# Two-stage fused attention and two-layer MLP: the order of all parts written out letter by letter

## Chip, cores and metric

The kernel runs on one core of one Trainium2 chip. The metric is the device time of one execution in microseconds, lower is better. Before the change it is 1310.85 us, the median of 3 runs (1309.78 to 1312.3).

## The reference, cut to what matters

`x` has shape (8, 8, 512, 64) and `state` (8, 8, 32, 64), both float32; the weights are float64 in memory.

```python
scores = scale * x @ state^T;  a = softmax(scores);   xread = a @ state
scores2 = scale * state @ x^T; a2 = softmax(scores2); sread = a2 @ x
t = concat([xread, sread], axis=2) as 4608 tokens of 512
h = (t @ w1) * (t @ w2) @ w3          # (512,1024), (512,1024), (1024,1024)
y = h @ w_out                          # (1024,512)
g = y @ w_in2; g = g - tanh(g)         # (512,2048)
out = g @ w_out2                       # (2048,512)
```

## The kernel before

**Stages.** Eight blocks `b` of 512 tokens hold what x reads, and a ninth (8) of 256 tokens what the state reads. Up to stage 2 there are four kinds of work. *Decoding* turns a float64 weight, read as two 32-bit words, into float32 (`unpack_abs` L343 and mostly `unpack_tail` L346 on ScalarE; `unpack_clamp`, `unpack_shift`, `unpack_end` L362 to L380 on VectorE; some tails on VectorE too). *The w3 products* multiply w3 and w_out: 16 items `t`, each with four turns on TensorE (`w3_turn` L771), a copy on ScalarE (L840), and four products with 512 columns (`w3_mul` L780; the first eight items need item `j` of both weights decoded). *Attention* (`attn_parts` L458): turn x, scores, two softmaxes, `sread`. *Folds* (`fold` L917) multiply the state by w1 and w2; the results go to DRAM (`fold_store` L952) and come back per block and `k` as `m` (`load_m` L1009). *Stage 1* (`stage1` L1036) multiplies `m` by the attention weights, *stage 2* (`stage2` L1069) the result by the w3 products. Stages 3 and 4 (L1295 to L1394) run after that in an order of their own, which the change leaves alone. Every stage matmul is done in three passes on a high and a low half.

**What sets the order.** Nothing is issued at once. Each helper calls `part` (L391), which puts a part on one of 13 streams with its engine (PE, ACT, DVE, SP), its cost in ns, what it needs and makes, and which ring of buffers it takes and gives back. `Plan.run` (L203) then makes eight rounds: `order` (L146) plays the streams by those costs and takes, for the engine that is free first, the part with the earliest due time; `justify` (L172) finds due times backwards. The round with the earliest end of PE is issued, part by part. Each engine executes its own parts strictly in that order, SyncE's DMA issues included, and `Plan.place` also picks the PSUM bank. The costs are `COST`, `WHOLE`, `TURN` (L36 to L42) and, for a change of kind on TensorE (turn, tiled for folds, scores and sread, whole for the rest), `SWITCH` (L45). DMAs are costed by their bytes.

**Around the change.** `units` (L799) says how w3 and w_out items 0 to 7 are decoded: items 0 and 1 one by one, then 2 and 3, 4 and 5, 6 and 7 in pairs. `load_xn` (L449) brings a block of x in four transfers of 256 KB, one for each `c`. The ring `m` has three buffers, `ph` four, `w3t` four; four PSUM banks `acc0` to `acc3` accumulate and four others are shared. The first TensorE instruction of the program is the turn of w3 item 0.

Of the kernel before, what the change touches and what calls it, by code (L numbers as in the profile page):

```python
# [18 lines left out]
P = 128  # L19
# [19 lines left out]
}  # L39
PASS = 226.7  # L40
WHOLE = 867.0
# [4 lines left out]
    ("whole", "tiled"): 91.0, ("turn", "tiled"): 91.0, ("tiled", "turn"): 97.0,  # L46
    ("tiled", "whole"): 230.0, ("turn", "whole"): 52.0, ("whole", "turn"): 10.0,
}


class Plan:
# [60 lines left out]
    def place(self, p, t):  # L112
# [5 lines left out]
        if p["bytes"]:  # L118
            self.moved = max(self.moved, end + 600) + p["bytes"] / 365.0
            end = self.moved + 2500  # L120
# [25 lines left out]
    def order(self):  # L146
        self.clear()
        found, lists = [], [list(s["parts"]) for s in self.streams]
        while any(lists):
            can = []  # L150
            for s, parts in zip(self.streams, lists):
                seen = set()
                for k, p in enumerate(parts[:s["ahead"]]):
                    if p["eng"] not in seen:
                        seen.add(p["eng"])
                        t = self.start(p)
                        if t is not None:
                            can.append((t, p["late"], parts, k, p))
            if not can:
                left = [parts[0] for parts in lists if parts]  # L160
                assert not left, [(p["eng"], p["need"], p["take"]) for p in left]
            t0, _, _, _, p0 = min(can, key=lambda c: c[0])
            t, _, parts, k, p = min(
                (c for c in can if c[4]["eng"] == p0["eng"] and c[0] <= t0 + self.NEAR),
                key=lambda c: (c[1] + self.CHANGE * (c[4]["kind"] not in (None, self.kind)), c[0]),
            )
            del parts[k]
            self.place(p, t)
            found.append(p)
        return found  # L170

    def justify(self, found):  # L172

        end = max(p["span"][1] for p in found)
        gaps = {e: [(0.0, end)] for e in self.REACH}
        bound = {id(p): end for p in found}
        for s in self.streams:
            last = {}
            for p in s["parts"]:
                if p["eng"] in last:  # L180
                    p["after"].append(last[p["eng"]])
                last[p["eng"]] = p
        late = {}
        for p in sorted(found, key=lambda p: -p["span"][1]):
            free = gaps[p["eng"]]
            k = next(
                (
                    k for k in reversed(range(len(free)))
                    if min(free[k][1], bound[id(p)]) - free[k][0] >= p["dur"]
                ),  # L190
                0,
            )
            a, b = free[k]
            t = min(b, bound[id(p)]) - p["dur"]
            free[k:k + 1] = [(a, t), (t + p["dur"], b)]
            late[id(p)] = t
            for q in p["after"]:
                lag = q["lag"] if q["eng"] != p["eng"] or q["bytes"] else 0.0
                bound[id(q)] = min(bound[id(q)], t - lag)
        for p in found:  # L200
            p["late"] = late[id(p)]

    def run(self):  # L203
        for s in self.streams:
            for p in s["parts"]:
                p["late"] = s["rank"].get(p["eng"], 9) if p["rank"] is None else p["rank"]
        best = None
        for _ in range(self.ROUNDS):
            found = self.order()
            end = max(p["span"][1] for p in found if p["eng"] == "PE")  # L210
            if best is None or end < best[0]:
                best = end, [(p, p["banks"]) for p in found]
            self.justify(found)
        for p, banks in best[1]:
            self.picked += banks
            p["fn"]()
# [3 lines left out]
def tile_kernel(  # L220
# [160 lines left out]

    plan = Plan()
# [8 lines left out]
    def part(stream, eng, cost, fn, need=(), make=(), take=(), give=(), size=0, rank=None, kind="whole"):  # L391
        if isinstance(cost, tuple):
# [21 lines left out]

    acc = {}

    def bank(t, name):
        acc[t] = pacc.tile([P, 512], F32, tag=f"acc{t}", name=name)

    with ExitStack() as actx:  # L420
# [28 lines left out]
        def load_xn(b):  # L449
            if b < B:  # L450
                t = pt.tile([P, NC, H, D], F32, tag="xn", name=f"xn{b}", bufs=2)
                xn[b] = t.rearrange("p c h d -> p c (h d)")
                for c in range(NC):
                    nc.sync.dma_start(
                        t[:, c], x[b].rearrange("h (p c) d -> c p h d", c=NC)[c]
                    )

        def attn_parts(b):  # L458
# [146 lines left out]
            def p(eng, cost, f, v=(), need=(), make=(), take=(), give=(), size=0, kind="turn"):  # L605
                part(
                    a_s, eng, cost, later(f, *v), [(b, *n) for n in need], [(b, *n) for n in make],
                    [(t, (b, *k), u) for t, k, u in take], [(b, *g) for g in give], size,
# [9 lines left out]
            if b == 0:  # L618
                p("SP", 3500, load_xn, (0,), (), [("xn",)], [("xn", ("xn",), KT + G)], (), 1 << 20)
# [22 lines left out]
            for j in range(G):  # L642
                p("DVE", full, by_head, (j,), [("sc", j)], [("a", j)], [("xt", ("a", j), 1)])
                p("DVE", 900, max2, (j,), [("sc", j)], [("m2", j)])
                p("ACT", 900, exp2, (j,), [("m2", j), ("a", j)], [("e", j)])
# [11 lines left out]
            for j in range(G):  # L657
                p("DVE", 1100, sum1, (j,), [("ex", j)])
# [8 lines left out]
                p("DVE", 330, whole2, (j,), [("e", j)], [("r2", j)])  # L667
                p("DVE", full, lo, (j,), [("hi", j)], [("at", j)], (), [("at32", j)])
            for j in range(G):
# [5 lines left out]
                    "DVE", 230, srtake, (j,), [("sr", j), ("r2", j)], [("srb", j)],  # L675
                    [("srb", ("srb",), 1)] if j == 0 else (), [("sr_ps", j)],
                )
            if b + 1 < B:
                part(
                    a_s, "SP", 3500, later(load_xn, b + 1), [], [(b + 1, "xn")],  # L680
                    [("xn", (b + 1, "xn"), KT + G)], (), 1 << 20,
# [14 lines left out]
        for b in range(B):  # L696
            if b % 4 == 0:
                r = b // 4
                part(
                    f_s, "SP", 4900, later(load_rows, r), [], [("zst", r)],  # L700
                    [("zst", ("zst", r))], (), 1 << 18,
# [78 lines left out]
        def w3_mul(t):  # L780
            h, j = divmod(t, nj)
            v = w3v[t]
            for a in range(4):
# [15 lines left out]
        units = [(half, (i,)) for i in range(2) for half in range(2)]  # L799
        units += [(half, (i, i + 1)) for i in range(2, nj, 2) for half in range(2)]  # L800
        f32_of = {(half, i): ("f32", half, items) for half, items in units for i in items}
        for u, (half, items) in enumerate(units):
            for i in items:
                part(
                    w_s, "SP", 450, later(fetch, i, half), (), [("raw", i, half)], (), (), 1 << 19
                )
        for t in range(2 * nj):
# [19 lines left out]
            if t in (0, 1, nj, nj + 2):  # L827
                u = nj + (t if t < nj else t // 2 - 2)
                part(
                    w_s, "SP", 450, later(fetch, u, 0), (), [("raw", u, 0)],  # L830
                    [("praw", ("praw", u))], (), 1 << 20,
# [4 lines left out]
                [("w3x", ("w3x", t), 1), ("w3t", ("w3t", t))],  # L836
# [6 lines left out]
            part(  # L843
                x_s, "PE", 4 * WHOLE, later(w3_mul, t),
                [("w3t", t), f32_of[1, j]], [("mul", t)],
                [(f"acc{a}", ("w3o", h, a), 2) for a in range(4)] if j == 0 else (), [("w3t", t)],
            )
            if j == nj - 1:
                for a in range(4):
                    part(  # L850
                        x_s, "ACT", ("scalar", 512), lambda h=h, a=a: copy(*w3_slice(h, a)[1::-1]),
                        [("mul", t)], [("w3oh", h, a)], (), [("w3o", h, a)],
# [15 lines left out]
        part(x_s, "SP", 0, open_pa, [("mul", 2 * nj - 1)], ["pa"])  # L868
# [27 lines left out]
        for k in range(NK):  # L896
# [5 lines left out]
            for h in range(2):  # L902
                part(
                    d_s, "SP", 450, later(w12_fetch, k, h), need, [("raw12", k, h)], (), (), 1 << 19
# [52 lines left out]
        for r in range(B // 4):  # L957
# [8 lines left out]
            for kk in range(NK // 2):  # L966
                for q in range(KT):
# [7 lines left out]
                    for j in range(G):  # L975
# [16 lines left out]
                        for l in range(2 if r else 1):  # L992
                            l = l if r else 1
                            part(
                                f_s, "SP", 550, later(fold_store, *f, j, l),
                                [(("fh", "fl")[l], *f, j)], [("mdr", *f, j, l)], (),
                                [("fe", *f, j, l)], 1 << 18,
# [95 lines left out]
        for b, k in steps:  # L1093
            n = S if b < B else NSR
            z = (b, k)
            if b < B:
                part(
                    m_s, "SP", 1950, later(load_m, b, k),
# [4 lines left out]
                    [("m", b, k) if b >= 4 else ("mw", b, k)], [("m", ("m", b, k), 2)], (),  # L1103
                    1 << (19 if b >= 4 else 18),
# [48 lines left out]
            for os in ((0, 1), (2, 3)):  # L1153
# [5 lines left out]
                if k == NK - 1:  # L1159
                    for o in os:  # L1160
# [6 lines left out]
                            s2, "SP", 450, later(y_store, b, o), [("yt", b, o)], [("ydr", b, o)],  # L1167
                            (), [("yt", b, o)], 1 << 18,
# [26 lines left out]
        for u in range(len(units)):  # L1195
            part(
                v_s, "SP", 450, later(w2_fetch, u), [("t12", NK - 1), ("s1", 2, 7, 1)], [("raw2", u)],
                [("raw", ("raw2", u))], (), 1 << 19,
# [6 lines left out]
                u_s, "SP", 450, later(w2_store, u), [("t2", u)], [("w2dr", u)], (), [("dt2", u)],  # L1205
                1 << 18,
# [53 lines left out]
        for d in range(10):  # L1260
            part(
                t_s, "SP", 450, w2_load, ["px"] + [("w2dr", u) for u in (range(2 * d, 2 * d + 2) if d < 8 else range(len(units)))],
# [165 lines left out]
```

## Time and profile before

| what | us |
|---|---|
| median of 3 runs | 1310.85 |
| the profiled execution | 1311.09 |
| its span, first to last instruction | 1309.0 |
| TensorE matmul busy | 1282.2 (98%) |
| VectorE busy | 955.8 (73%) |
| ScalarE busy | 742.5 (57%) |

A timeline row has the start in us from the span's start, the duration, the engine, the line, the operation, output and inputs, shapes, how many instructions were merged, and in brackets the idle time before it with what ended it. PE is TensorE's matmuls, DVE VectorE, ACT ScalarE, SP SyncE (all DMA issues here). Durations of merged matmuls include the last one's drain, so the time that a run of matmuls takes from the engine is better read from its start to the next row's start.

### The profile page before, as it was taken

What the parts mean: (1) busy time and instruction counts of PE and PEld (TensorE: products, weight loads), DVE (VectorE), ACT (ScalarE), POOL (GpSimd) and SP (SyncE); (2) the same over time, 40 slices, a digit from 0 to 9 for tenths busy, and PEclk for the clock granted to TensorE, in tenths of its full rate; (3) what the DMA queues carried; (4) which work ended last, traced back from release to release, by engine and by line L of the source; (5) the groups of instructions that cost most, each with busy time, mean ns of one, the idle gap of its engine ahead of it and who ended that gap; (6) DMA issues with size and microseconds to landing.
All of it is one profiled execution on the core that took longest, in us unless ns stands there. A gap on an engine that the chain in (4) does not pass through costs nothing.

```text
span 1309.0 us, 17283 instructions
## 1 busy us (share of the span) xinstructions
PE 1282.2 (98%) x6352; PEld 1010.7 (77%) x6352; DVE 955.8 (73%) x1578; ACT 742.5 (57%) x1188; POOL 0.7 (0%) x6
## 2 busy tenths in 40 slices
PE   6999999999999999999999999999999999999998
PEld 3445667777777788888888888888888888888887
DVE  7788575685576863569787687786877877768777
ACT  7895564566666764456555454554554545545444
POOL 0000000000000000000000000000000000000000
PEclk9999999999999999999999999999999999999999
DMA  9975674659879735630010100100101001001000
GB/s 320 328 234 156 215 239 124 210 164 262 256 215 255 206 116 177 193 129 33 1 65 1 58 8 1 65 1 1 65 1 65 1 1 65 1 1 49 1 33 17
DMA packets 111747, 141.63 MB, mean 108 GB/s; under 512 B 43824, under 2 KB 81712, under 8 KB 109616
## 3 DMA queue, kind: packets, MB, share of 16 engines
q1 hardware_dynamic: 111664, 140.55, 34.9%
q8 instruction: 50, 0.82, 0.3%
q14 instruction: 33, 0.27, 0.1%
HBM read 89.13 MB, written 51.38 MB: 107 GB/s over the span
## 4 chain that ended last, share of the span: by engine, by line
PE 84%; DVE 5%; DMA 5%; ACT 3%; SPq 1%; issue 1%; DVEq 0%; ACTq 0%
PE h_ps L325 27%; PE o_ps L1346 27%; PE ab_ps L325 13%; PE y_ps L1077 12%; PE m_ps L923 2%; PE w3o_ps L787 2%; DMA m<-mdr 1%; DMA w2dr_in<-dt_w 1%; PE x_ps L317 1%; DMA raw_p<-in_moe_w_out_dram 1%; DMA raw_p<-in_moe_w_dram 1%; DMA raw<-in_moe_w_dram 0%; SPq L1016 0%; PE sr_ps L572 0%; PE sc_ps L478 0%
## 5 line engine op out<-in xcount | busy, mean ns | idle before, releaser
L325 PE MATMUL h_ps<-yt,w2in 128*128 128x512 f32 (+1 forms) x1728 | 394.0, 377 | 0.0
L325 PEld LDWEIGHTS h_ps<-yt,w2in 128*128 128x128 f32 x1728 | 313.5, 188 | 61.0
L1077 PE MATMUL y_ps<-ph,w3o 128*128 128x512 f32 (+1 forms) x864 | 202.2, 381 | 0.0
L325 PE MATMUL ab_ps<-at,m 128*128 128x512 f32 x768 | 191.4, 396 | 2.1 <-DMA m<-mdr 1.1
L1077 PEld LDWEIGHTS y_ps<-ph,w3o 128*128 128x128 f32 x864 | 154.2, 188 | 35.8 <-issue 6.4
L325 PEld LDWEIGHTS ab_ps<-at,m 128*128 128x128 f32 x768 | 140.8, 188 | 42.8 <-issue 3.6
L295 ACT ACTIVATE ph<-ac 128x512 fp32r<-128x512 f32 (+1 forms) x72 | 43.9, 609 | 82.4 <-PE y_ps L1077 70.3
L298 DVE TENSOR_TENSOR ph<-ac,ph 128x512 fp32r<-128x512 f32 (+1 forms) x72 | 47.4, 658 | 58.6 <-ACT ph L295 57.9
L787 PE MATMUL w3o_ps<-wo,w3t 128*128 128x512 f32 x128 | 60.7, 623 | 3.5 <-ACT w3t L295 3.5
L1060 DVE TENSOR_TENSOR ac<-ab_ps,ac 128x512 f32<-128x512 f32 (+1 forms) x72 | 47.2, 656 | 18.1 <-PE ab_ps L325 15.7
L787 PEld LDWEIGHTS w3o_ps<-wo,w3t 128*128 128x128 f32 x128 | 24.4, 199 | 33.4 <-issue 28.9
L295 ACT ACTIVATE ac<-ab_ps 128x512 f32<-128x512 f32 (+1 forms) x72 | 40.5, 563 | 10.7 <-PE ab_ps L325 10.7
L353 ACT ACTIVATE raw_w<-raw_w 128x512 uint16<-128x512 uint32 x32 | 43.8, 1370 | 0.7
L923 PE MATMUL m_ps<-raw,uu 64*128 64x512 f32 x128 | 38.0, 651 | 3.9 <-DVE raw L377 2.4
L1356 DVE COPY ob<-o_ps 128x512 f32<-128x512 f32 x17 | 11.8, 692 | 39.1 <-PE o_ps L1346 39.1
L295 ACT ACTIVATE fe<-m_ps 128x512 fp32r<-128x512 f32 (+1 forms) x48 | 27.8, 599 | 15.1 <-PE m_ps L923 14.2
L295 ACT ACTIVATE ob<-o_ps 128x512 f32<-128x512 f32 x17 | 10.2, 599 | 45.1 <-PE o_ps L1346 45.1
L298 DVE TENSOR_TENSOR fe<-m_ps,fe 128x512 fp32r<-128x512 f32 x32 | 21.2, 683 | 12.0 <-ACT fe L295 10.7
L377 DVE SCALAR_TENSOR_TENSOR dt_w<-raw_w,dt_w 128x512 uint32<-128x512 uint32 x32 | 22.1, 691 | 10.3 <-ACT raw_w L353 10.1
L298 DVE TENSOR_TENSOR w2in<-w2lin,w2in 128x1024 fp32r<-128x1024 f32 x8 | 9.8, 1223 | 24.5 <-ACT w2in L295 24.4
L344 ACT ACTIVATE dt_w<-raw_w 128x512 f32<-128x512 f32 x32 | 21.2, 662 | 11.3 <-DMA w2dr_in<-dt_w 5.3
L298 DVE TENSOR_TENSOR m<-m 128x512 fp32r<-128x512 f32 x32 | 21.8, 684 | 6.9 <-ACT m L295 6.9
(1818 smaller groups left out, 2305.1 us busy)
## 6 DMA issues: line engine op xcount, KB each, us to landing
mdr<-fe SPq DMA_DIRECT2D x96, 256.0 KB, 2.7
m<-mdr SPq DMA_DIRECT2D x128, 128.0 KB, 4.4
xn<-in_x_dram SPq DMA_DIRECT2D x32, 256.0 KB, 4.9
raw<-in_moe_w_dram SPq DMA_DIRECT2D x16, 512.0 KB, 8.4
m<-mdr SPq DMA_DIRECT2D x128, 64.0 KB, 2.1
ydr<-y SPq DMA_DIRECT2D x32, 256.0 KB, 3.4
raw_w<-in_moe_w_in_dram SPq DMA_DIRECT2D x16, 512.0 KB, 5.0
raw_w<-in_moe_w_out_dram SPq DMA_DIRECT2D x16, 512.0 KB, 5.4
```

The lines of the kernel that those rows point to most:

```text
L295: nc.scalar.activation(dst, src, AF.Copy)
L298: nc.vector.tensor_tensor(out=lo, in0=src, in1=hi.bitcast(F32), op=ALU.subtract)
L317: nc.tensor.transpose(dst[:, i * P:(i + 1) * P], s, ident)
L325: nc.tensor.matmul(out_ap, lhs(i), rhs(j), start=(n == 0), stop=(n == m - 1))
L344: nc.scalar.activation(t.bitcast(F32), word(raw, 1).bitcast(F32), AF.Abs)
L353: nc.scalar.activation(tail, word(raw, 0), AF.Copy, scale=TAIL)
L377: nc.vector.scalar_tensor_tensor(out=t if to is None else to, in0=word(raw, 1), scalar=0xC0000007, in1=t, op0=ALU.bitwise_and, op1=ALU.bit ...
L787: nc.tensor.matmul(acc[a], v[:, a * P:(a + 1) * P], wo[:, j].bitcast(F32), start=(j == 0), stop=(j == nj - 1),)
L923: nc.tensor.matmul(ts[j].rearrange("p (k h f) -> p k h f", k=2, h=2), uu[r][1][d, q * P:(q + 1) * P], w[d, :, :, q], start=True, stop=True ...
L1060: nc.vector.tensor_tensor(out=ab[b, k], in0=ab[b, k, 1], in1=ab[b, k], op=ALU.mult)
L1077: nc.tensor.matmul(acc[o][:, :n], w3o[k // 4][:, k // 2 % 2, i, c + o * P:c + (o + 1) * P], p[:, j], start=(k == 0 and e == 0), stop=(k == ...
L1346: nc.tensor.matmul(acc[t], g[:, i, t * P:(t + 1) * P], w[:, l, c], start=(f == 0 and e == 0), stop=(f == NF - 1 and e == 2),)
```

## The change

1. `order`, `justify` and the rounds go. `run` reads a string of 1907 letters, `ORDER`: each letter names a stream and an engine, and the next part of that pair is placed and issued. PSUM banks are still picked by `place`, by costs that are now single numbers for each kind of transfer (`MOVE`) and finer for changes of kind.
2. `load_xn` becomes one transfer of 1 MB.
3. Before anything else TensorE makes 36 turns of the identity into the bank `acc3`; nothing reads them.
4. Items 0 to 3 of w3 and w_out are decoded one by one (`SINGLE`), and the transfers are issued in that order.
5. The four products of an item become two parts of two, which the order may set apart.

```diff
+WARM = 36
+SINGLE = 4
+ENGINES = ("PE", "ACT", "DVE", "SP")
+LETTERS = "abcdefghijklmnopqrstuvwxyzABCDEFGHIJKLMNOPQRSTUVWXYZ"
+ORDER = (
+    "lllllllllljlljklkljlkljkmlkhjknkjqkkjkjkqkkjklmkxjkxnkxjqkxdkjkkqkkkjmkmnkkjqkkxxkqxnkxjqkjkmjmk"
...
+    "LINKNXZKHYHGIZGBILGLNNKGHHIXGIXYKXYZXGYYKZKHHIXKIXYKHHIZXKYXYKYZKGKIHKIKKKKLLNNLNLN"
+)
...
+    def run(self):
         self.clear()
-        found, lists = [], [list(s["parts"]) for s in self.streams]
...
+        left = {
+            (i, e): [p for p in s["parts"] if p["eng"] == e]
+            for i, s in enumerate(self.streams) for e in ENGINES
+        }
+        assert len(ORDER) == sum(map(len, left.values()))
+        for letter in ORDER:
+            i, e = divmod(LETTERS.index(letter), len(ENGINES))
+            p = left[i, ENGINES[e]].pop(0)
+            t = self.start(p)
             self.place(p, t)
...
+            self.picked += p["banks"]
             p["fn"]()
...
+    bank(3, "warm_ps")
+    for i in range(WARM):
+        nc.tensor.transpose(acc[3][:, i % 4 * P:(i % 4 + 1) * P], ident, ident)
...
-                for c in range(NC):
-                    nc.sync.dma_start(
-                        t[:, c], x[b].rearrange("h (p c) d -> c p h d", c=NC)[c]
-                    )
+                nc.sync.dma_start(t, x[b].rearrange("h (p c) d -> p c h d", c=NC))
...
-        def w3_mul(t):
+        def w3_mul(t, s):
...
-            for a in range(4):
+            for a in range(2 * s, 2 * s + 2):
...
-        units = [(half, (i,)) for i in range(2) for half in range(2)]
-        units += [(half, (i, i + 1)) for i in range(2, nj, 2) for half in range(2)]
+        units = [(half, (i,)) for i in range(SINGLE) for half in range(2)]
+        units += [(half, (i, i + 1)) for i in range(SINGLE, nj, 2) for half in range(2)]
```

The 13 streams, in the order that the letters count them: attention (`a` to `d` for its PE, ACT, DVE, SP), folds (`e` to `h`), decoding of w3 and w_out (`i` to `l`), turns of w3 (`m`, `n`), w3 products (`q` to `t`), w1 and w2 (`v` to `x`), loads of m (`z`, `A`, `B`), its halves (`D`, `E`), stage 1 (`G` to `I`), stage 2 (`K`, `L`, `N`), decoding of stage 3's weights (`P` to `R`), their fetches (`V`), and their way back (`X` to `Z`). So the first 34 letters spell, for SyncE, the fetches w3 0, w_out 0, w3 1, w_out 1 and on; for ScalarE abs and tail of w3 0, abs and tail of w_out 0, abs of w3 1, the copy of item 0's turns and abs of w_out 1; and last TensorE's `q`, the first half of product 0.

## Rows read from the trace of the kernel before

**Rows 1.** Stretches: length, busy us of PE, PEld, DVE, ACT, POOL, then PEclk, DMA, GB/s:
```profile
0.00:7.00 7.00, 0.00 (x0) 0.00 (x0) 1.49 (x5) 3.99 (x5) 0.70 (x6) 1.00 0.76 254
7.00:17.00 10.00, 7.51 (x12) 3.38 (x13) 7.12 (x14) 6.44 (x7) 0.00 (x0) 1.00 1.06 374
...
40.00:105.00 65.00, 60.42 (x286) 28.14 (x284) 53.50 (x81) 56.45 (x67) 0.00 (x0) 1.00 0.86 268
105.00:562.00 457.00, 451.49 (x2627) 350.90 (x2626) 288.35 (x536) 270.17 (x459) 0.00 (x0) 1.00 0.67 197
562.00:1309.00 747.00, 742.02 (x3362) 617.52 (x3360) 585.54 (x921) 386.92 (x635) 0.00 (x0) 1.00 0.08 29
```

**Rows 2.** TensorE's waits from 0 to 105 us: us in total, times, longest:
```profile
PE w_ps L317 <- DVE w3f L377: 8.3, 2, 7.3
PE w3o_ps L787 <- ACT w3t L295: 3.5, 2, 2.2
PE m_ps L923 <- DVE raw L377: 2.4, 1, 2.4
```

**Rows 3.** Timeline of TensorE, turns and w3 products: start, us, engine, line, count:
```profile
7.29 1.08 PE L317 MATMUL w_ps<-ident,w3f 128*128 128x128 f32 x4 [7.29 <-DVE w3f L377]
10.57 6.64 PE L787 MATMUL w3o_ps<-wo,w3t 128*128 128x512 f32 x8 [2.20 <-ACT w3t L295]
...
28.00 1.04 PE L317 MATMUL w_ps<-ident,w3f 128*128 128x128 f32 x8
...
67.06 3.60 PE L787 MATMUL w3o_ps<-wo,w3t 128*128 128x512 f32 x8
...
101.83 3.70 PE L787 MATMUL w3o_ps<-wo,w3t 128*128 128x512 f32 x8
```

**Rows 4.** Timeline of ScalarE and of SyncE's x loads, 0 to 73 us:
```profile
4.39 0.66 ACT L344 ACTIVATE w3f<-raw_p 128x512 f32<-128x512 f32 x1 [2.16 <-DMA raw_p<-in_moe_w_dram]
5.08 1.34 ACT L353 ACTIVATE raw_p<-raw_p 128x512 uint16<-128x512 uint32 x1
...
9.36 0.67 ACT L344 ACTIVATE wo<-raw_p 128x512 f32<-128x512 f32 x1 [0.35 <-DMA raw_p<-in_moe_w_out_dram]
9.94 0.58 ACT L295 ACTIVATE w3t<-w_ps 128x512 f32<-128x512 f32 x1
...
14.83 2.50 ACT L353 ACTIVATE raw_p<-raw_p 128x1024 uint16<-128x1024 uint32 x1
...
62.31 1.17 ACT L344 ACTIVATE dt_p<-raw_p 128x1024 f32<-128x1024 f32 x1 [1.64 <-DMA raw_p<-in_moe_w_dram]
...
24.04 7.36 SPq L454 DMA_DIRECT2D xn<-in_x_dram  x4
```

**Rows 5.** Stretches around the one fall of TensorE's clock, columns as in rows 1:
```profile
129.50:133.00 3.50, 3.50 (x17) 2.51 (x14) 2.34 (x4) 1.64 (x3) 0.00 (x0) 0.56 0.64 219
133.00:136.00 3.00, 3.00 (x16) 1.70 (x15) 0.00 (x0) 1.75 (x5) 0.00 (x0) 1.00 0.26 94
```

**Rows 6.** Timeline of TensorE: turns, a fold visit between stage parts, the last run:
```profile
130.49 1.97 PE L317 MATMUL x_ps<-ident,xn 128*128 128x128 f32 x8
...
163.90 1.52 PE L1077 MATMUL y_ps<-ph,w3o 128*128 128x512 f32 x6
165.35 1.13 PE L923 MATMUL m_ps<-raw,uu 64*128 64x512 f32 x4
166.41 1.65 PE L1077 MATMUL y_ps<-ph,w3o 128*128 128x512 f32 x6
...
544.43 17.84 PE L1077 MATMUL y_ps<-ph,w3o 128*128 128x512 f32 x78
```

**Rows 7.** The m loads: issue ns min/median/max; landing:
```profile
L1016 SPq DMA_DIRECT2D m<-mdr x256: 302/419/1590, 77.1 to 533.2; - x128
...
DMA to landing us min/median/max: 1.8/2.9/8.9
```

**Rows 8.** SyncE's waits: us in total, times, longest:
```profile
SPq L1016 <- PE ab_ps L325: 52.8, 27, 5.0
```

More of the change, by code (lines that the diff above doesn't have):

```diff
@@ L39 @@
 }
+MOVE = {
[6 rows of a table added]
+}
 PASS = 226.7
-WHOLE = 867.0
+WHOLE = 859.0
 TURN = 109.0
 SWITCH = {
-    ("whole", "tiled"): 91.0, ("turn", "tiled"): 91.0, ("tiled", "turn"): 97.0,
-    ("tiled", "whole"): 230.0, ("turn", "whole"): 52.0, ("whole", "turn"): 10.0,
-}
+    ("stage", "tiled"): 91.0, ("turn", "tiled"): 94.0, ("whole", "tiled"): 93.0,
+    ("tiled", "stage"): 220.0, ("tiled", "turn"): 154.0, ("tiled", "whole"): 198.0,
+    ("turn", "stage"): 34.0, ("whole", "stage"): 130.0, ("stage", "turn"): 5.0,
+}
@@ L118, in place @@
         if p["bytes"]:
-            self.moved = max(self.moved, end + 600) + p["bytes"] / 365.0
-            end = self.moved + 2500
+            _, begin, share, land = p["bytes"]
+            self.moved = max(self.moved, t + begin) + share
+            end = self.moved + land
         reach = end + self.REACH[p["eng"]]
@@ L144, in place @@
             self.made[n] = (max(at, reach), by + [p])
-    def order(self):
+    def run(self):
         self.clear()
-        found, lists = [], [list(s["parts"]) for s in self.streams]
[L149 to L165, printed above, removed]
-            )
-            del parts[k]
-            self.place(p, t)
-            found.append(p)
-        return found
@@ L172, in justify @@
[L172 to L215, printed above, removed]
+        left = {
+            (i, e): [p for p in s["parts"] if p["eng"] == e]
+            for i, s in enumerate(self.streams) for e in ENGINES
+        }
@@ L216, in run @@
+        assert len(ORDER) == sum(map(len, left.values()))
[3 more added lines that the diff above has]
+            t = self.start(p)
+            assert t is not None, (p["eng"], p["need"], p["take"])
+            self.place(p, t)
+            self.picked += p["banks"]
             p["fn"]()
@@ L389, in tile_kernel, with part @@
         plan.ring(name, n)
-    def part(stream, eng, cost, fn, need=(), make=(), take=(), give=(), size=0, rank=None, kind="whole"):
-        if isinstance(cost, tuple):
+    def part(stream, eng, cost, fn, need=(), make=(), take=(), give=(), rank=None, kind="stage"):
+        size = 0
+        if isinstance(cost, str):
+            size = MOVE[cost]
+            cost = size[0]
+        elif isinstance(cost, tuple):
             kind, n = cost
@@ L603, in sr_lo, with p @@
                 low(xsr[:, q:q + 2], at[B][:, 0, q:q + 2], at[B][:, 1, q:q + 2])
-            def p(eng, cost, f, v=(), need=(), make=(), take=(), give=(), size=0, kind="turn"):
+            def p(eng, cost, f, v=(), need=(), make=(), take=(), give=(), kind="turn"):
                 part(
                     a_s, eng, cost, later(f, *v), [(b, *n) for n in need], [(b, *n) for n in make],
-                    [(t, (b, *k), u) for t, k, u in take], [(b, *g) for g in give], size,
+                    [(t, (b, *k), u) for t, k, u in take], [(b, *g) for g in give],
                     rank=3 if b == 0 and eng != "PE" else None, kind=kind,
@@ L804, in tile_kernel @@
                 part(
-                    w_s, "SP", 450, later(fetch, i, half), (), [("raw", i, half)], (), (), 1 << 19
+                    w_s, "SP", "words", later(fetch, i, half), (), [("raw", i, half)]
                 )
@@ L842, in tile_kernel @@
             )
[L843 to L847, printed above, removed]
+            for s in range(2):
+                part(
+                    x_s, "PE", 2 * WHOLE, later(w3_mul, t, s),
+                    [("w3t", t), f32_of[1, j]], [("mul", t, s)],
+                    [(f"acc{a}", ("w3o", h, a), 2) for a in range(2 * s, 2 * s + 2)]
+                    if j == 0 else (),
+                    [("w3t", t)], kind="whole",
+                )
             if j == nj - 1:
@@ L866, in open_pa @@
             )
-        part(x_s, "SP", 0, open_pa, [("mul", 2 * nj - 1)], ["pa"])
+        part(x_s, "SP", 0, open_pa, [("mul", 2 * nj - 1, s) for s in range(2)], ["pa"])
         def w12_fetch(k, h):
```

83 lines of the change are left out of this document (49 added, 34 removed), and 6 rows, old and new, of the table MOVE.

## The prediction

> **What bounds the kernel now.** I read the stretches first, then TensorE's waits, then its timeline at the start, and last the other engines' timelines there. In the stretches, TensorE is busy 742.0 of 747 us from 562 us on [rows 1]; that is stages 3 and 4, which the change leaves alone. From 105 to 562 us it idles 457.0 - 451.5 = 5.5 us [rows 1]. Before 105 us it idles the first 7.0 us, 2.5 us of the next 10, and 4.6 us of the 65 from 40 us on [rows 1]. The waits say for what: 8.3 us for decoded w3 (7.3 of it before the first instruction), 3.5 us for ScalarE's copies of turned w3, 2.4 us for decoded w1/w2 [rows 2]. In that stretch ScalarE is busy 56.5 of 65 us [rows 1], and up to 17 us DMA moves 374 GB/s [rows 1]. So TensorE's own work bounds nearly everything, and all that an order can win lies in TensorE's waits, its changes of kind, and the time in which its clock was low.
>
> The clock shows in durations. The granted clock reads 1.00 from the start [rows 1], yet the first product takes 6.64 us for eight matmuls and a later one 3.60; four turns take 1.08 and later eight take 1.04 [rows 3]. [...]
>
> **The change, part by part.** The sum is made against the profiled execution, 1311.09 us, 0.24 above the median of 1310.85; its span is 1309.0.
>
> *36 turns first.* They need only the identity, there by about 1.5 us. At the lower level eight turns take 1.97 us [rows 6], 0.25 each; at the upper 1.04 [rows 3], 0.13. So 36 take between 4.7 us (all fast) and 9.0 us (all slow), and end between 6.2 and 10.5 us. I take a rise part of the way, and an end near 8 us. The first real turn started at 7.29 [rows 3]; about a microsecond of delay is covered, since ScalarE copies its result only after the abs of w3 1, at 9.3 us (below). Without that cover it would cost the whole microsecond. If the clock is up, product 0 takes 3.60 in place of 6.64: 3.0 us gained, and 0.5 on its turns. Do turns raise the clock? In the low stretch TensorE ran, from 130.49 us, eight turns of x in 1.97 us [rows 6], and the clock was back at 133 [rows 5]: turns were most of what it did before the rise. [...]
>
> *The decoding of items 0 to 3 one by one, and the new order of the first 65 us.* I walked the letters with the durations of the rows. ScalarE: abs of w3 0 at 4.39, then tail, abs, tail, abs, copy: 0.66 + 1.34 + 0.67 + 1.34 + 0.67 + 0.58 [rows 4] = 9.65, with hand-overs 9.95. Product 0 starts there, in place of 10.57 [rows 3]. Then abs of w_out 1. The fourth transfer landed just before 9.36 [rows 4]; each further 0.524 MB takes 1.40 us at 374 GB/s [rows 1], so w3 2 is there at 10.8 and w3 3 at 13.6. Abs and tail of w3 2, abs of w_out 2, abs of w3 3, copy: 14.9. Product 1 then starts 1.0 us after TensorE could have. Items 2 to 8 go on in this way, with pairs at 1.17 and 2.50 us on ScalarE [rows 4]; I find waits of 0.65, 0.65, 0.2, 0.9, and 0.85 and 0.3 behind the turns of x. By the end of product 10 TensorE has done eleven products of 3.5, twelve turns of w3, one of the state and four of x at 0.44, three folds and the scores at 1.06 [rows 3, 6]: 38.5 + 7.5 + 4.2 = 50.2 us. The waits, 9.5 us at the start among them, add 14.1: 64.3 us. Before, product 10 ended at 67.06 + 3.60 = 70.7 [rows 3] with 0.4 us more done. The lead is 70.7 - 0.4 - 64.3 = 6.0 us; about 3.5 of it is the clock. I take 5.5, for hand-overs that I left out. The transfers allow it: w3 items of the second half wait for their landing at 62.31 now [rows 4], but are fetched ahead of most of w1 and w2 in the letters. After 65 us ScalarE's parts up to the last tail of w1/w2 sum to some 36 us and TensorE's to about as much, so the lead is kept up to the last product, which ended at 105.5 [rows 3], and no more. Bounds: 2.5 us if TensorE waits on ScalarE as much as now; 7.5 if nothing is lost in hand-overs.
>
> *Changes of kind.* A fold between stage parts takes 1.06 from start to start, and the edges beside it 1.45 - 1.37 and 1.49 - 1.37 more (1.37 is six of the 78 matmuls in 17.84) [rows 6]: 0.2 us a visit. I count 46 visits to folds, scores and sread now, 35 of them after 105 us, and 40 in the letters, 32 of them after the last product. Those before are in the walk; three fewer save 0.6 us.
>
> *After 105 us.* If no idle time like that before 129.5 us comes, the low clock there goes too: half of 3.5 us, 1.7. Of 5.5 us of waits [rows 1] the new order may lose all or have them again elsewhere; I take 3.5 left, so 2.0 saved, between 0 and 4.5.
>
> *x in one transfer.* Four issues hold SyncE for 7.36 us behind full queues [rows 4], and later m loads of 1.7 us each (four issues of 0.42 [rows 7]) stand behind them. A single issue costs SyncE between one of these and all of it; bytes and element size stay. Nothing waits for SyncE at the first x, since eight w1/w2 fetches are ahead or behind it in a full DMA queue; I take 0, with bounds of -1 and +1 us.
>
> *Two-part products.* The same instructions; a part more on no queue but TensorE's: 0, covered by the walk.
>
> Sum: 5.5 + 0.6 + 1.7 + 2.0 = 9.8; 1311.1 - 9.8 = 1301.3, against the median 1301.0.
>
> **Rivals.** (1) *Turns do not raise the clock.* Then the 36 end at 10.5 us less a little, the first turns after them are slow, product 0 starts some 0.9 us later and takes 3.0 more: 1301.0 + 3.9 = 1305. The rows of 130 us speak against it [rows 5, 6]. (2) *ScalarE and VectorE take the gain back.* They are busy 56.5 and 53.5 of 65 us [rows 1] with the same parts in both orders. If the folds, softmax and decoding crowd so that TensorE waits as now, and the later waits stay, 2.5 + 0.6 is left: 1308. For it: these shares. Against it: ScalarE's idle time at the start, which the walk fills. (3) *Slower: SyncE's fixed order holds m loads back.* SyncE executes its letters strictly; today it stands 27 times, 52.8 us in all, until TensorE frees an m buffer [rows 8], and everything behind it stands too. An m load takes 1.7 us to issue and 2.9 to land, 8.9 at most [rows 7]. In the letters the tightest loads (block 3 and block 5, late k) have four stage parts of 1.37 and a turn, 5.9 us, between issue and reader; eleven have under 8.5. Where the 1 MB of x or w2 stores stand ahead and the landing goes to 8.9, such a load costs 10.6 - 7 = 3.6 us. It decides from three such loads; with five the time is 1301 + 18 = 1319. Against it: now only 5.5 us of all waits lie in that stretch. (4) *It changes nothing*: the letters spell nearly what the planner found, and waits move rather than vanish: 1311.
>
> **How the numbers follow.** The forecast, 1296 to 1306, gets 0.66; (1) 0.10, (2) 0.12, (3) 0.08, (4) 0.04. The low end is 1311.1 - (7.5 + 0.6 + 1.7 + 4.5) - 1 = 1296 at the bounds, and 1295 with a little for them; the high end takes in (1) and (2), 1308. Left out are (3), (4) and the edges. What a measurement of this kernel can tell from no change is about 0.2%, 2.6 us. (1) and nearly all of (2) are faster by more, a sliver of (2) is not: faster 0.86, same 0.06, slower 0.08.
>
> **What would show it.** The start: 36 turns from about 1.5 us, their spacing halving on the way; product 0 near 10 us and in 3.6 us. Product 10 ending near 65, the last w3 product near 99 to 100 with its neighbours' work done, h_ps starting near 552 instead of 562. TensorE's waits after the last product near 3.5 us, no stretch at 0.5 of the clock inside, eight issues of x. I am wrong if product 0 takes over 6 us, if the ScalarE waits of TensorE between 40 and 105 us are above 4.6, or if waits on m loads sum to several microseconds.

## The result, and the profile after

The changed kernel took 1296.05 us (median of 4 runs, 1292.31 to 1296.95) against 1311.57 us for the kernel before (4 runs, 1309.78 to 1312.31): a ratio of 0.9878, with a 95% interval of 0.9856 to 0.9901. That is 15.5 us less; forecast were 10. The profiled execution is the fastest of the four, 1292.31 us with a span of 1290.5, 18.5 us below the span of before.

Stretches of the changed kernel, the last cut a little behind the start of its stage 3 (543.69 us), columns as in [rows 1]:
```profile
0.00:7.00 7.00, 5.60 (x36) 5.36 (x36) 1.33 (x5) 3.96 (x5) 0.70 (x6) 1.00 0.74 253
...
40.00:105.00 65.00, 63.71 (x309) 29.05 (x307) 54.61 (x85) 56.29 (x72) 0.00 (x0) 1.00 0.89 264
105.00:548.00 443.00, 442.81 (x2612) 351.16 (x2613) 286.42 (x531) 267.60 (x454) 0.00 (x0) 1.00 0.70 205
```
From 40 to 105 us TensorE now idles 1.3 us in place of 4.6, though ScalarE and VectorE are as busy as before [rows 1]. From 105 to 548 us it idles 0.2 us; before, from 105 to 562, it was 5.5.

All of TensorE's listed waits in the changed kernel, over the whole span: us in total, times, longest:
```profile
PE w3o_ps L778 <- ACT w3t L281: 3.0, 3, 1.4
PE warm_ps L375 <- POOL ident masks.py:199: 1.4, 1, 1.4
PE m_ps L917 <- ACT fe L281: 1.2, 1, 1.2
PE w_ps L303 <- DVE dt_p L363: 0.8, 1, 0.8
PE w_ps L303 <- DVE w3f L363: 0.7, 2, 0.4
PE ab_ps L311 <- ACT y L281: 0.2, 1, 0.2
PE o_ps L1338 <- ACT g(8, 15)_11177 L281: 0.2, 1, 0.2
```
Of the 7.3 us before the first instruction [rows 2], 5.6 are filled with turns of the identity, the wait for decoded w1/w2 is gone, and no wait on an m load is left.

The timeline of TensorE in the changed kernel, to be held against [rows 3]:
```profile
1.36 5.60 PE L375 MATMUL warm_ps<-ident 128*128 128x128 f32 x36 [1.36 <-POOL ident masks.py:199]
...
9.39 3.70 PE L778 MATMUL w3o_ps<-wo,w3t 128*128 128x512 f32 x8 [1.37 <-ACT w3t L281]
...
59.48 5.42 PE L778 MATMUL w3o_ps<-wo,w3t 128*128 128x512 f32 x12
...
92.40 1.13 PE L917 MATMUL m_ps<-raw,uu 64*128 64x512 f32 x4 [1.18 <-ACT fe L281]
...
94.49 2.22 PE L917 MATMUL m_ps<-raw,uu 64*128 64x512 f32 x4
96.64 1.66 PE L311 MATMUL ab_ps<-at,m 128*128 128x512 f32 x6
...
543.69 1.52 PE L311 MATMUL h_ps<-yt,w2in 128*128 128x512 f32 x6
```
Product 0 starts at 9.39 us in place of 10.57 and takes 3.70 in place of 6.64. Product 10 is the first eight of the twelve matmuls at 59.48, so it ends near 59.48 + 8 x 5.42/12 = 63.1 us, in place of 70.7. The last half product starts at 89.34 and ends near 91.2; the last product ended at 105.5 before. Stage 3 (h_ps) begins at 543.69; before, in the same view:
```profile
562.12 2.20 PE L325 MATMUL h_ps<-yt,w2in 128*128 128x512 f32 x9
```
From there both kernels need the same time (1290.5 - 543.69 = 746.8; 1309.0 - 562.12 = 746.9). So the whole gain, 18.4 us in this pair, lies before h_ps, and I split it at the last matmul of the last w3 product, in the changed kernel and before:
```profile
90.64 0.59 PE L778 MATMUL w3o_ps<-wo,w3t 128*128 128x512 f32 x1
```
```profile
104.94 0.59 PE L787 MATMUL w3o_ps<-wo,w3t 128*128 128x512 f32 x1
```
It starts 14.3 us earlier. But behind it the changed kernel has more of other work still to do: by the instructions in the two traces three folds, twelve turns and six matmuls of stage 1, which is 3 x 1.06 + 12 x 0.109 + 6 x 0.227 = 5.9 us at the spacing from start to start that these have in a run. From there to h_ps, before needs 457.2 us and the changed kernel 453.1, of which 453.1 - 5.9 = 447.2 go to work that before has there too. **The lead at the last product is worth 14.3 - 5.9 = 8.4 us, and the rest of stage 2 saves 457.2 - 447.2 = 10.0 us.** The pair has the fastest execution of the changed kernel in it; a second trace of that kernel (below) gives 8.1 and 8.3.

The list of waits above does not hold everything. The fold at 94.49 takes 2.15 us to the next matmul where the others take 1.06: its two halves, which elsewhere run side by side (the four matmuls take 1.13 us; the two of one half alone, at 126.81 before, take 1.12), run one behind the other, the second behind a copy by ScalarE, as the row of its weight loads (PEld) shows. Before, the fold at 124.31 lost as much in the same way: its second half starts 2.50 us after the first, and 1.38 of that is a listed wait.
```profile
95.58 0.29 PEld L917 LDWEIGHTS m_ps<-raw,uu 64*128 64x128 f32 x2 [0.80 <-ACT fe L281]
```

### The profile page after: what moved, and what is told of

It reads as the page before. It is cut to its first block, busy times and chain, and to the rows that moved or that the text cites. A ratio compares the mean times of both kernels' runs of the same rounds, so it can differ in the third digit from the quotient of the medians.

```text
span 1290.5 us, 17382 instructions
## 1 busy us (share of the span) xinstructions
PE 1278.2 (99%) x6388; PEld 1013.4 (79%) x6388; DVE 956.4 (74%) x1585; ACT 740.8 (57%) x1191; POOL 0.7 (0%) x6
## 4 chain that ended last, share of the span: by engine, by line
PE 93%; DVE 3%; ACT 2%; DMA 1%; issue 0%; SPq 0%; DVEq 0%; ACTq 0%
PE h_ps L311 27%; PE o_ps L1338 27%; PE ab_ps L311 16%; PE y_ps L1071 15%; PE m_ps L917 3%; PE w3o_ps L778 2%; DMA raw_p<-in_moe_w_out_dram 1%; PE x_ps L303 1%; PE sr_ps L563 1%; PE sc_ps L469 1%; ACT raw_p L339 1%; PE et_ps L303 1%; DVE h_ps L1310 0%; PE w_ps L303 0%; SPq L740 0%
## 5 line engine op out<-in xcount | busy, mean ns | idle before, releaser
L1071 PE MATMUL y_ps<-ph,w3o 128*128 128x512 f32 (+1 forms) x864 | 198.6, 382 | 0.0
L311 PE MATMUL ab_ps<-at,m 128*128 128x512 f32 x768 | 186.7, 393 | 0.2 <-ACT y L281 0.2
L778 PEld LDWEIGHTS w3o_ps<-wo,w3t 128*128 128x128 f32 x128 | 22.7, 190 | 29.6 <-issue 24.7
L284 DVE TENSOR_TENSOR fe<-m_ps,fe 128x512 fp32r<-128x512 f32 x32 | 21.6, 687 | 14.9 <-ACT fe L281 8.9
L350 DVE TENSOR_SCALAR dt_w<-dt_w 128x512 f32<-128x512 f32 x32 | 13.5, 422 | 24.0 <-ACT dt_w L330 23.6
```

Source lines behind the costliest of these rows:

```text
L284: nc.vector.tensor_tensor(out=lo, in0=src, in1=hi.bitcast(F32), op=ALU.subtract)
L311: nc.tensor.matmul(out_ap, lhs(i), rhs(j), start=(n == 0), stop=(n == m - 1))
L778: nc.tensor.matmul(acc[a], v[:, a * P:(a + 1) * P], wo[:, j].bitcast(F32), start=(j == 0), stop=(j == nj - 1),)
L1071: nc.tensor.matmul(acc[o][:, :n], w3o[k // 4][:, k // 2 % 2, i, c + o * P:c + (o + 1) * P], p[:, j], start=(k == 0 and e == 0), stop=(k == ...
```

## The experiments

Eleven runs, each compared with the kernel before on the same chip. "Letters" is the written-out order of the 1907 parts; "parts" are the change's other edits.

**The changed kernel again.** No edit. In question: what makes its runs differ by 4.6 us.

> The changed kernel once more, nothing edited. Theory: its time is 1292 to 1297 us and the spread comes from the clock: the 36 turns run from 1.4 us, the clock rises at a place of its own in each execution, and an execution that is 3 to 4 us longer shows a stretch at 0.5 of the clock somewhere between 20 and 540 us, with TensorE's waits as before (about 7 us in all). Rival: the spread comes from transfers: the clock is the same, and TensorE's waits sum to 3 us more.

1295.57 us (1294.29 to 1296.44), ratio 0.9881 [0.9868 to 0.9894], span of the profiled execution 1292.5. The line among TensorE's waits that is new:
```profile
PE ab_ps L311 <- DMA m<-mdr: 1.3, 2, 0.7
```
and in its timeline products 0 and 2:
```profile
9.26 3.70 PE L778 MATMUL w3o_ps<-wo,w3t 128*128 128x512 f32 x8 [1.25 <-ACT w3t L281]
...
20.57 5.42 PE L778 MATMUL w3o_ps<-wo,w3t 128*128 128x512 f32 x12 [1.42 <-ACT w3t L281]
```
The theory fell: the granted clock is no lower than in the first execution (mean 1.000 against 0.999), so the clock does not make the 2.0 us between these two. Nor does it make the 3.5 to 4 us between three of the first four runs: those of 1292.31, 1295.84 and 1296.27 us all have a mean granted clock of 0.999, and a thousandth of the clock over the span is 1.3 us (an estimate from these figures). Of the 2.0 us by which h_ps comes later (545.70), 0.3 are there at the last product and 1.3 are waits for m loads to land. In the traces of the six kernels below that have these letters, with one or two moved at most, the waits for m loads sum to between 0.7 and 4.8 us; how much of that is the edit and how much the execution, one trace each can't say.

**The change without the 36 turns, and the kernel before with them.**
```diff
-WARM = 36
+WARM = 0
```


> The changed kernel without the 36 turns. Theory A (the term of my sum): product 0 runs at the lower clock, over 6 us instead of 3.7, and the whole loss of 3.5 us reaches the end: about 1299.5 us. Theory B (walk with ScalarE's queue): product 0 is as slow, but ScalarE idles 2.6 us at 15.9 us and TensorE waits 0.9 and 0.8 us at 20 and 37 us, and these take up most of the delay: 0.5 to 1.5 us more than the changed kernel. Rival C: no difference, since the clock would be up without the turns.

1297.1 us (1295.98 to 1300.59), ratio 0.9898 [0.9883 to 0.9913], 1.5 us above the changed kernel of the same chip; the intervals overlap, so the times alone do not settle whether the turns are worth 0 or 3 us. Its timeline of TensorE:
```profile
9.24 5.21 PE L778 MATMUL w3o_ps<-wo,w3t 128*128 128x512 f32 x8 [0.92 <-ACT w3t L281]
...
21.01 3.27 PE L778 MATMUL w3o_ps<-wo,w3t 128*128 128x512 f32 x7 [0.85 <-ACT w3t L281]
```
Product 0 is slow again, by 1.5 us, but product 2 starts only 0.4 us later than in the changed kernel (21.01 against 20.57 in the second trace): in between TensorE waits for ScalarE's copies, 1.25, 1.03 and 1.42 us in that trace, and behind the slow product 0.92, 0.69 and 0.85. The last w3 product comes 0.4 to 0.7 us later than in the two traces of the changed kernel (91.37 against 90.95 and 90.64). That is what theory B expected. The other run puts the turns, and nothing else, into the kernel before:
```diff
+    bank(3, "warm_ps")
+    for i in range(36):
+        nc.tensor.transpose(acc[3][:, i % 4 * P:(i % 4 + 1) * P], ident, ident)
+
     plan = Plan()
```


> The kernel before with the 36 turns alone. Theory A (the clock is worth what it saves on the first product): 3 us less than before, about 1308.5 us. Theory B: in the old order the next copy of turned w3 stands behind a tail of 2.5 us on ScalarE and starts at about 18 us whatever TensorE does, so product 1 starts at 18.7 instead of 19.1 and only 0.3 to 0.6 us of 3 reach the end, about 1311.

1311.6 us (12 runs, 1309.6 to 1315.0), ratio 1.001 [0.9999 to 1.002]: nothing. Its timeline of TensorE, then its stretches, columns as in [rows 1]:
```profile
10.74 5.40 PE L791 MATMUL w3o_ps<-wo,w3t 128*128 128x512 f32 x8 [2.81 <-ACT w3t L295]
...
18.86 1.11 PE L317 MATMUL w_ps<-ident,w3f 128*128 128x128 f32 x4 [2.28 <-DVE w3f L377]
19.77 4.87 PE L791 MATMUL w3o_ps<-wo,w3t 128*128 128x512 f32 x8
```
```profile
12.20:15.60 3.40, 3.40 (x6) 1.37 (x5) 1.54 (x3) 1.67 (x2) 0.00 (x0) 0.52 1.06 371
...
19.00:22.40 3.40, 3.40 (x8) 1.85 (x9) 3.33 (x4) 2.89 (x2) 0.00 (x0) 0.51 1.09 360
```
The 36 turns do their work here too: the four turns of w3 behind them take 0.66 us, 1.08 without them [rows 3]. But the granted clock falls to 0.52 and 0.51 in the two stretches above, which come behind waits of 2.81 and 2.28 us that the old order leaves open, and the first two products take 5.40 and 4.87 us, where 3.60 is seen later [rows 3]; product 1, behind the turn at 18.86, starts at 19.77 and not at 18.7 as expected. In the old order the turns gain nothing.

**Twice as many turns.**
```diff
-WARM = 36
+WARM = 72
```


> The changed kernel with 72 turns of the identity in place of 36. Theory: 36 more turns at 0.109 us hold the first turn of w3 back by 3.9 us, to about 11.3; ScalarE's copy waits with it, and the waits at 14, 20 and 37 us take up a part: 1 to 2.5 us above the changed kernel. Rival: everything behind is bound by TensorE, and the whole 3.9 us reach the end: 1299.5 us.

1298.45 us (1296.34 to 1300.63), ratio 0.9903 [0.989 to 0.9917], 2.9 above the changed kernel. Product 0 starts at 12.89 us, 3.6 later than in the second trace of the change (9.26), and product 2 at 22.54, 2.0 later: the waits for copies take up nearly half of a delay at the start. The last w3 product is then 2.0 us later too. The trace is of the slowest of the five runs, 1300.63 us, and has 4.8 us of waits for m loads, 3.5 more than the second trace of the change; how much of the 2.9 us between the medians they make, it can't say.

**x in four transfers again**, all else as changed.
```diff
-                nc.sync.dma_start(t, x[b].rearrange("h (p c) d -> p c h d", c=NC))
+                for c in range(NC):
+                    nc.sync.dma_start(
+                        t[:, c], x[b].rearrange("h (p c) d -> c p h d", c=NC)[c]
+                    )
```


> The changed kernel with x in four transfers of 256 KB again. Theory: no difference, within 1 us of the changed kernel, since SyncE's queue is ahead of what TensorE needs. Rival: three more issues a block hold SyncE, stage 1 waits for m, and the time is 2 to 6 us above it, with waits of ab_ps on m in the list of waits.

1297.03 us (1295.65 to 1298.37), ratio 0.9893 [0.988 to 0.9905]: 1.5 us more than the changed kernel, between its theory and its rival, but the intervals overlap, and the run does not settle whether a single transfer is worth 0 or 2 us. SyncE's timeline at the first x in the changed kernel, with one issue where before four took 7.36 us [rows 4]:
```profile
30.40 2.12 SPq L447 DMA_DIRECT2D xn<-in_x_dram  x1
32.64 11.37 SPq L871 DMA_DIRECT2D raw<-in_moe_w_dram  x4
```
And in the run with four issues, the same stretch:
```profile
31.78 8.80 SPq L448 DMA_DIRECT2D xn<-in_x_dram  x4
40.69 2.73 SPq L874 DMA_DIRECT2D raw<-in_moe_w_dram  x4
```
One issue of x and the four fetches behind it hold SyncE from 30.40 to 44.01 us; four issues of x and the same four fetches from 31.78 to 43.42. What the single issue gives back, the next ones take.

**All parts of the change, ordered by the old planner.** The two-part products, the single items, x in one and the turns are in; letters and new costs are not. The edit, against the changed kernel:
```diff
-ORDER = (
...
-        for letter in ORDER:
...
+        for _ in range(self.ROUNDS):
+            found = self.order()
...
+            self.justify(found)
```


> All of the change but the letters: 36 turns, x in one transfer, items 0 to 3 one by one, products in two parts, the order by the old planner and its costs. Theory: the order carries nearly everything, so this stays at 1306 to 1311 us (up to 4 us from the single items, none from the turns, as the turns alone gained none). Rival: with finer parts any planner feeds TensorE better, and most of the 15 us is here too: 1302 us or less.

1320.23 us (1315.41 to 1324.94), ratio 1.0069 [1.0047 to 1.0091]: 9 us slower than before, and both expectations missed. TensorE's waits, and its timeline at the worst place:
```profile
PE m_ps L927 <- ACT fe L295: 5.3, 2, 3.7
...
PE w3o_ps L788 <- DVE w3o L298: 3.5, 2, 3.4
```
```profile
53.92 1.13 PE L927 MATMUL m_ps<-raw,uu 64*128 64x512 f32 x4 [3.10 <-issue]
...
62.59 3.68 PE L788 MATMUL w3o_ps<-wo,w3t 128*128 128x512 f32 x4 [3.37 <-DVE w3o L298]
```
With finer parts the old planner, which takes the next part by its due time, turns to folds and `sread` early, and no w3 product runs between 50 and 62.6 us. The clock falls too: over the execution its granted mean is 0.995, against 0.999 in the changed kernel, and it is 0.50 in two stretches that come right behind the waits of 3.37 and 3.67 us. Behind a third wait, of 3.07 us, four matmuls at 10.93 take 3.32 us, where four at 18.75 take 1.88. The two stretches, columns as in [rows 1]:
```profile
62.60:66.00 3.40, 3.40 (x4) 1.48 (x5) 1.38 (x3) 3.37 (x4) 0.00 (x0) 0.50 1.06 377
76.30:79.70 3.40, 3.40 (x9) 1.74 (x8) 3.31 (x6) 2.75 (x5) 0.00 (x0) 0.50 0.48 160
```
How the 9 us divide between waits and clock, no run shows. The parts by themselves, with the old planner and its costs, are a loss here; the gain is the order's.

**The letters for one half.** One kernel takes the first 319 letters, up to the last w3 product, and plans the rest in eight rounds as before, with the changed costs; the other plans up to the last product and places the rest by the letters.
```diff
+PREFIX = 319
...
+        for letter in ORDER[:PREFIX]:
...
+        while any(lists):
+            can = []
...
```


> The changed kernel with the letters up to the last part of product 15 (319 of 1907), and the old planner's eight rounds for all parts behind. Theory: the head brings the lead of 7.9 us that the two traces show at the last product, and the tail pays the old planner's waits of 5 us and its visits again: 1301 to 1305 us, with TensorE's waits after 105 us at 4 to 6 us. Rival: the head is all that counts and the tail fills itself: within 2 us of the changed kernel, 1294 to 1298.

```diff
+        head = [p for p, _ in best[1]]
+        last = max(n for n, p in enumerate(head) if p in self.streams[4]["parts"] and p["eng"] == "PE")
...
+        for letter in ORDER:
+            i, e = divmod(LETTERS.index(letter), len(ENGINES))
+            p = left[i, ENGINES[e]].pop(0)
+            if id(p) not in used:
+                rest.append(p)
```


> The reverse: the old planner up to the last part of product 15, with all parts of the change, then the letters for what is left. Theory: the tail brings what the head does not, some 7 us, so 1301 to 1305 us, TensorE's waits after the last product under 2 us. Rival: an order for the tail is worth something only behind the head that it was written for: waits of 4 us and more, 1306 us or above.

The first: 1302.37 us (1301.97 to 1303.75), ratio 0.9936 [0.9924 to 0.9948]. The second: 1314.9 (12 runs, 1306.84 to 1317.79), ratio 1.0028 [1.0012 to 1.0043]. Against the old planner with the same parts, the letters of the head are worth 1320.2 - 1302.4 = 17.9 us, those of the rest 1320.2 - 1314.9 = 5.3; together 23.2 of the 24.7 us that all letters gained (the medians of two chips; the kernel before differs by 0.4 between them). The first also plans with the changed costs and the old planner's run does not, so the 17.9 are not the letters' alone.

The second missed its theory (1301 to 1305) and came out where its rival put it, at 1306 or above. Yet the two traces do not bear out that rival's reason, that the rest of the letters is worth little behind another head. Up to the last product both run the same instructions on TensorE in the same order, and behind it they have the same work: it takes 457.0 us by the planner (from 115.33 to 572.33) and 447.6 by the letters (117.14 to 564.79), 9.4 us less. What differs besides is the head: the same order ends 1.8 us later in the second trace, with slow matmuls in other places (six from 63.52 take 5.38 us, by the planner from 62.59 4.54; a fold at 56.13 takes 2.08, by the planner at 56.15 1.13; four matmuls of a product at 80.37 take 2.86, by the planner at 79.36 2.05), while at the start it is the planner's that are slow (3.32 us for four at 10.93, 1.98 at 9.98 in the second trace). The mean granted clock is 0.995 in both. The runs of these two spread over 9.5 and 11 us, so the 5.3 from medians, and the sum of 23.2, are rough.

The time of the first was as expected; its waits were not. TensorE's waits in it behind the last product (of 92 us and later), and its first h_ps:
```profile
PE m_ps L982 <- ACT fe L346: 1.2, 1, 1.2
PE et_ps L368 <- ACT sc L558: 1.0, 2, 0.7
PE m_ps L982 <- DVE ac L1119: 0.6, 1, 0.6
PE ab_ps L376 <- DVE fe L349: 0.6, 1, 0.6
PE ab_ps L376 <- ACT ac L346: 0.2, 1, 0.2
```
```profile
553.34 1.98 PE L376 MATMUL h_ps<-yt,w2in 128*128 128x512 f32 x8
```
From the last product to h_ps it takes 8.7 us longer than the changed kernel for the same work, and only 2.2 of that is in listed waits (3.6 us against the 1.2 and 0.2 of the changed kernel in that part). Some 4.2 is in matmuls of stages 1 and 2 that start a little later than back to back (it changes 101 times between the two stages, the changed kernel 63 times), and about 1.3 in six more visits to folds, scores and sread; that the changes of stage make the late starts is my reading, no run separates it. The list of waits shows a quarter of the 8.7 us.

**Two listed waits taken away by one letter each.** The fold at 92.40 waits 1.18 us for ScalarE. In the first kernel one letter of ScalarE (r, a copy of the summed products of w3's second half) moves behind the copy that the fold waits for; in the second the copy of w3 2 moves ahead of the abs of the pair 4, 5; the third does both.
```diff
-    "qfcvhcwhebBwvcqgccwfeDhwrhaagfqbwhbwhDretr...
+    "qfcvhcwhebBwvcqgccwfeDhwhaagfqbwhbrwhDretr...
```


> One letter moved: ScalarE's first copy out of the last w3 product (w3oh of half 1) goes behind its copy of fold 0.1.3, the state's and the first of x. In the changed kernel ScalarE idles 2.9 us at 88.4 us for that product while TensorE then waits 1.2 us for the fold's copy behind it. Theory: what is left of waits in the head are such single places of the order, so TensorE's wait of 1.2 us goes and the time falls by 0.8 to 1.2 us (1294.5). Rival: behind it waits something else (the transfers of m for block 0), the wait moves to ab_ps or x_ps, and the time stays within 0.4 us.

```diff
-    "...kkjkjkqkkjklmkxjkxnkxjqkxdkjkkqkkkjmkmnkkjqkk...
+    "...kkjkjkqkkjklmkxjkxnkxjqkxdkjkkqkkkmkmnjkkjqkk...
```


> One letter moved: ScalarE's copy of turned w3 2 goes ahead of its abs of the pair w3 4 and 5, which waits 2.6 us for its landing at 18.5 us while the turns are done at 18.2. Theory: product 2 starts at 19.1 to 19.3 us instead of 20.2 to 20.6, and since TensorE is bound from there on 0.5 to 1.1 us reach the end. Rival: the pairs behind are bound by transfers and VectorE, TensorE waits a microsecond more for the turns at 25 or 37 us, and nothing reaches the end.

> Both letters moved. Theory: the gains add, 1.3 to 2.3 us below the changed kernel, about 1293.8. Rival (each place is covered by another): within 0.5 us of it.

In order: 1295.8 us (1295.36 to 1297.97), ratio 0.9893 [0.9879 to 0.9906]; 1297.6 (1296.55 to 1299.89), 0.9904 [0.989 to 0.9917]; 1294.38 (1292.53 to 1295.99), 0.9878 [0.9864 to 0.9891]. The changed kernel on the other chip has 0.9881 [0.9868 to 0.9894]; none of the three can be told apart from it. The first one's timeline and waits:
```profile
95.97 1.67 PE L311 MATMUL ab_ps<-at,m 128*128 128x512 f32 x6
```
```profile
PE ab_ps L311 <- DMA m<-mdr: 3.3, 2, 2.0
```
The wait is gone and the first ab_ps comes at 95.97 in place of 96.94 us (the changed kernel's second trace), but 3.3 us are then spent waiting for m loads. The second kernel's timeline of TensorE:
```profile
19.23 3.70 PE L778 MATMUL w3o_ps<-wo,w3t 128*128 128x512 f32 x8
23.23 1.98 PE L778 MATMUL w3o_ps<-wo,w3t 128*128 128x512 f32 x4 [0.29 <-ACT w3t L281]
...
28.37 3.70 PE L778 MATMUL w3o_ps<-wo,w3t 128*128 128x512 f32 x8 [0.57 <-ACT w3t L281]
...
37.72 0.63 PE L303 MATMUL w_ps<-ident,dt_p 128*128 128x128 f32 x4 [0.91 <-DVE dt_p L363]
38.18 3.60 PE L778 MATMUL w3o_ps<-wo,w3t 128*128 128x512 f32 x8
```
Product 2 starts 1.3 us earlier (20.57 in the changed kernel's second trace), and 18 us later everything is where it was (38.18 against 38.31): three waits of 0.29, 0.57 and 0.91 us have taken it back (only the last of them, with 0.69, is there without the move).

## Why the prediction was right, and where its sizes were off

The sign held, and so did the range, by little and with some luck: 1296.05 us lies at the very edge of the forecast 1296 to 1306, and the second measurement's 1295.57 below it, within the 1295 to which the prediction stretches its low end. The forecast of 10 us was short of 15.5 by medians, and of 18.4 in the profiled pair. Nor does the range set the rivals apart, since the 1305 of rival (1) lies in it; the rows do. By the prediction's own steps:

- **The start.** The walk put product 0 at 9.95 us and product 1 at 14.9; measured 9.39 and 14.21. The turns raised the clock, as far as durations show it: with nothing run but turns of the identity, their spacing halves, which the stretches of the changed kernel show for those instructions alone (length, PE busy and count, PEld busy and count, clock, DMA, GB/s):
```profile
1.36:4.30 2.94, 2.94 (x14) 2.94 (x15) 1.00 0.80 254
4.30:7.00 2.70, 2.65 (x24) 2.42 (x22) 1.00 1.05 379
```
  That is 0.21 us a turn and then 0.11, and product 0 takes 3.70, in place of 5.21 without the turns. The granted clock reads 1.00 in both stretches, as it does while product 0 takes 6.64 us before [rows 1, 3]; what it shows later is 0.56 where eight turns take 1.97 us [rows 5, 6]. Rival (1) falls for this form of turn (128x128, f32). What I had wrong was the price of the clock: I put 3.5 us of the head's lead down to the clock. Without the turns the changed kernel is 1.5 us slower by medians, which its spread does not set apart from nothing, and 0.4 to 0.7 us behind at the last product; with them the old kernel gains nothing.
- **The head lead, 5.5 us: it measured 8.4.** This is the first term that was mis-sized. By the end of product 10 the walk had 64.3 us and the trace has 63.1. The last matmul of that product starts at 62.58 in place of 70.07, with one set of four turns less of other work done (0.44 us, as in the walk), so that the lead there is 70.07 - 62.58 - 0.44 = 7.0 us, where I walked 6.0 and took 5.5 "for hand-overs". What was off is the waits: 4.6 us forecast from product 0's start on, 2.7 measured. The other 1.4 us come after: I wrote that "the lead is kept up to the last product", and no more, but before, a turn waited 1.1 us there for a copy (at 73.84), and that wait is gone.
- **After the last product, 0.6 + 1.7 + 2.0 = 4.3 us: it measured 10.0.** This is the second mis-sized term, and the larger one. The longest of TensorE's waits before, from 105 to 562 us:
```profile
PE m_ps L923 <- DVE srb L582: 1.4, 1, 1.4
PE et_ps L317 <- ACT sc L502: 1.4, 1, 1.4
PE ab_ps L325 <- DMA m<-mdr: 1.1, 2, 0.9
PE ab_ps L325 <- DVE ac L1060: 0.8, 1, 0.8
```
  Of 5.1 us of listed waits before (5.5 of idle time), I left 3.5; the first trace has 1.4 left (1.2 of it the fold at 92.40) and the second 2.5, so they are worth 3.7 and 2.6 in place of 2.0. The granted clock is 1.00 from 105 to 548 us, so no fall of it remains, which is the 1.7 us forecast (before, it was 0.76 from 128.8 to 129.5 us and 0.56 from there to 133 [rows 5], and the instructions between lost about that much; that idle time had brought it was my reading). Visits to folds and the like went from 34 to 32 by the rows, where I had counted 35 and 32: some 0.4 us in place of 0.6. What I did not cost at all is the small change: TensorE goes 63 times straight from one of stages 1 and 2 to the other in place of 100, and about 2.8 us of starts a little later than back to back are gone. Some 1.4 us of the 10.0 I can't assign.
- **ScalarE and VectorE take it back** (rival 2): they do absorb what happens in the first 20 us (the 1.5 us of product 0 without the 36 turns are 0.4 at product 2, the 3.6 with 72 are 2.0, and the 1.3 us that the moved copy brings product 2 are 0.1 at 38 us), but in the changed order TensorE idles only 1.3 us in all from 40 to 105.
- **SyncE's fixed order holds m loads back** (rival 3): the waits are there, at 0 to 4.8 us from trace to trace and not at 18. SyncE stands 28 times, 52.8 us in all, until TensorE frees an m buffer, 27 times and as long before [rows 8], and an m load takes 3.3 us from issue to landing in the median of the changed kernel, 2.9 before [rows 7]. The waits set where in the 4.6 us spread an execution falls, I think; shown is that those waits differ between traces of the same letters. A fourth m buffer would be the test; it was not tried.
- **x in one transfer, 0 with bounds of 1; two-part products, 0.** The first stays open between 0 and 2. The second was not tried alone; all parts together, with the old planner, cost 9 us.

That an order could be forecast at all before it ran rests on one thing: its letters can be walked with the durations of the old trace. The walk came out within 1.2 us at 63. Where I did not walk, the sizes were off: 0 for 1.4 us from there to the last product, and 4.3 for 10.0 behind it, where I only took a share of the waits.

## What to carry to other kernels

Judge an order by how far the work has come at a fixed point, and not by the waits that it removes: of 8.7 us that the planner's second half cost against the letters, the list of waits showed 2.2, and two listed waits of over 1 us, taken away by one letter each, gave nothing that could be measured. Ask of a warm-up of TensorE what runs behind it: in the old order the clock that the turns had raised fell again, to a granted 0.52 and 0.51, and they gained nothing; in the new one it stayed up (1.00 in each stretch up to 548 us), and they are worth 1.5 us by medians, which the spread of the runs leaves open. The parts that the old planner turned into a loss of 9 us are in the faster kernel too: try parts and order together.

## What was not expected of the hardware

In the old kernel the clock that the 36 turns had raised fell again at 12.2 and at 19.0 us, behind waits of 2.81 and 2.28 us that ended at 10.74 and 18.86 (granted 0.52 and 0.51 in the stretches that follow), while in the changed kernel, with waits of up to 1.4 us in the same 25 us, it did not fall (granted 1.00 in every stretch). In the kernel with all parts and the old planner it was 0.50 right behind waits of 3.37 and 3.67 us. And executions of one and the same program differ in when transfers land: the waits for m loads were 0 and 1.3 us in two traces of the changed kernel, most of the 2.0 us between their first h_ps.
